# A windowed attention and two feed-forward layers on one core: where a softmax constant is added, which bank a product goes to, who issues two stores

## The chip, the cores and the metric

The kernel runs on one core of a Trainium2 chip. A core has a matrix engine (TensorE, PE in the profile, with its weight loads listed apart as PEld), three elementwise engines (VectorE or DVE, ScalarE or ACT, GpSimd or POOL) and SyncE (SP), which here only issues DMAs. Each engine works through its own queue of instructions in order. The metric is the device time of one execution in microseconds (us); the time before is the median of three runs.

## The reference: what is computed

All data is fp32. Attention over 4 batches, 8 heads, 576 positions, 64 values a head; each query sees the 128 keys up to its own, with a bias that falls with distance. The result, as 2304 rows of 512, goes through two layers.

```python
scores = scale * np.matmul(q, k.transpose(0, 1, 3, 2))
mask = (rel >= 0) & (rel < window)            # window = 128
scores = np.where(mask, scores + bias[None], -1000000000.0)
scores = scores - np.max(scores, axis=-1, keepdims=True)
attn = np.exp(scores)
attn = attn / (np.sum(attn, axis=-1, keepdims=True) + 1e-09)
x = np.matmul(attn, v)                        # rows (b, s), columns (h, d)
h = x @ w_in                                  # 512 x 2048
g = np.where(h > 0.0, h, np.exp(np.minimum(h, 0.0)) - 1.0)
x = g @ w_out                                 # 2048 x 512
h = x @ w_in_2
out = np.maximum(0.01 * h, h) @ w_out_2
```

The `1e-09` added to the sums is what the change's title calls the constant.

## The kernel before

**Products.** TensorE has to keep fp32 accuracy, so every product of a layer is three matmuls: both operands are split into a high and a low part (`fp32r`), and high x high, high x low and low x high are added in one accumulator (`split_mm`, whose matmul is line 120). The low part is what VectorE gets by subtracting the high part from the fp32 value: where av, the attention's result, lies in PSUM, ScalarE casts it to the high part (`values_cast`) and VectorE subtracts (`values_rest`). Both write `x`, the left operand of layer 1, and both read the bank that av lies in. The weights come as 64-bit words in pieces of 512 KB (`w_in`, `w_out`) and are converted to fp32 and split by ScalarE and VectorE (`wraw` is what was loaded, `wf` the first step of ScalarE, line 170, and `w` the result).

**Stages.** The attention is cut into steps: a step `s` is a pair of heads with up to two groups of queries (its `subs`, one or two) of a block of 256 rows. A step goes through `score_mm` (s_ps on TensorE), `score_min` (VectorE: bias, mask and maximum, the `stat` of the rows), `score_exp` (ScalarE: exp, with the row sums into `stat`), the constant, `score_rec` (VectorE: reciprocal), `score_norm` (GpSimd: the multiply `t<-t,stat`), `transposes` (TensorE into `pt_ps`, then ScalarE's copy to `pt`), `selects` (GpSimd: sets to zero what is outside the window) and `values` (TensorE: av_ps from `pt` and V).

In the opening, 16 steps (`FIRST`) run in an order written out by hand: while `Ordered.on` is set, every instruction of `act`, `dve` and `pool` keeps the order of the program on its engine. Round `n` has the transposes of step n, the products of step n - 1, the reductions, exp and constant of step n + 2, the selects of step n, and the multiply of step n + 1. Conversions of early weight pieces are mixed in on ScalarE and VectorE (`EARLY`).

After it, layer 1 runs over five blocks J of rows (512, 256, 512, 512, 512), each over 16 chunks c of 128 of the 2048 hidden values: `mlp1_h` (h_ps, 12 matmuls, then exp on ScalarE, and on VectorE a minimum, the maximum of line 522 that reads the bank last, and the subtract for the low part) and `mlp1_y` (the second product, two chunks later). At some chunks, the starts (at J = 0 chunks 3, 7, 11 and 15, then every other chunk from 0), two attention steps of a later block stand ahead of h_ps: their transposes, the values of the pair before, their selects and the scores of the next pair. After the last chunk of a block, `ys` copies (even pieces by ScalarE, odd ones by VectorE, in buffers `eg` that the chunks also use, three of them) go to DRAM as `x2T`, four stores of 256 KB. Layer 2 loads them again (`xr`), and its `mlp2_h` and `mlp2_y` run to the end; the `g` of its chunks (line 681) is made by ScalarE from h_ps, in the same `eg` buffers. The first chunks of layer 2 are mixed into the last block of layer 1, and the last two blocks' stores are issued by ScalarE, all others by SyncE.

**Order.** TensorE and the conversions of the weights keep the program's order. Outside the opening a scheduler puts the other instructions in order, and buffers of a pool are given out in turn: who asks for a buffer waits for the last reader of what lay in it.

**Banks.** PSUM has eight banks: s0 and s1 (scores; s1 also the first transposes of a start), h and c, y0 to y3. The second transposes of a start go into h, av of the late blocks into c (line 458), and h_ps alternates between h and c:

```python
        tag = "s0" if last and cs[0] < LAG2 and (LAG2 - cs[0]) % 2 else "h"
        if not last and cs[0] % 2 == (J == 0):
            tag = "c"
```

So before, the h_ps of a chunk with a start goes to c (even chunks from J = 1 on, odd ones at J = 0), and that of a chunk without one to h.

Of the kernel before, what the change touches and what calls it, by code (L numbers as in the profile page):

```python
# [84 lines left out]
def attention_elu_leaky_kernel(  # L85
# [262 lines left out]
    def score_exp(s):  # L348
        st = steps[s]
        t, stat = st["t"], st["stat"]  # L350
        for i, (t0, n, before, hh, c) in enumerate(st["reg"]):
            act.activation(t[:n, c], t[:n, c], AF.Exp, scale=-1.0,
                           bias=stat[:n, 0, i:i + 1], accum_out=stat[:n, 1, i:i + 1])
        nq, m = st["subs"][0][1], len(st["reg"])
        if Ordered.on:
            act.activation(stat[:nq, 1, :m], stat[:nq, 1, :m], AF.Copy, bias=1e-9)
        else:
            dve.tensor_scalar(stat[:nq, 1, :m], stat[:nq, 1, :m], 1e-9, None, op0=ALU.add)
# [12 lines left out]
    def scores(k):  # L371
# [5 lines left out]
        for s in (2 * k, 2 * k + 1):  # L377
            score_min(s)
            score_exp(s)
            score_rec(s)  # L380
            score_norm(s)
# [61 lines left out]
    def values(s):  # L443
# [17 lines left out]
        for t0, n, hh, k0, nk, c in st["parts"]:  # L461
            ch = [x[0] for x in chunks].index(k0)
            nth = sum(x[0] == -nk and x[2] == hh for x in mms)
            mms.append((-nk, nth, hh, ch, slice(t0 + off, t0 + off + n), c))


        mms.sort(key=lambda x: x[:3])
        for i, (nk, _, hh, ch, q, c) in enumerate(mms):
            matmul(av[hh * D:hh * D + D, q], v[:-nk, ch, hh * D:hh * D + D], pt[:-nk, c],
                   start=st["first"] and all(x[2] != hh for x in mms[:i]),  # L470
# [17 lines left out]
    def mlp1_h(J, cs, late_work=lambda: None):  # L488
# [8 lines left out]
        tag = "s0" if last and cs[0] < LAG2 and (LAG2 - cs[0]) % 2 else "h"  # L497
        if not last and cs[0] % 2 == (J == 0):

# [29 lines left out]
    def mlp1_y(J, cs, gg):  # L529
# [12 lines left out]
        if cs[-1] == NC - 1:  # L542
            for i, y in enumerate(Y.pop(J)):
# [5 lines left out]

                q = nc.sync if J < len(BLK1) - 2 else nc.scalar  # L550
                q.dma_start(out=x2T[:, i * per:i * per + per, t0:t0 + n], in_=ys)
# [36 lines left out]
    score_min(0)  # L588
    score_exp(0)
    score_min(1)  # L590
    score_rec(0)
    score_norm(0)
    score_exp(1)
    for n in range(FIRST):
        m = n + 2
# [7 lines left out]
        score_min(m)  # L603
        if n < FIRST - 2:
            score_norm(m - 1)
        score_exp(m)
        selects(n)
        if n >= FIRST - 2:
            score_norm(m - 1)
# [18 lines left out]
    for J in range(len(BLK1) - 1):  # L628
# [3 lines left out]
        for c in range(NC):  # L632
            if c in starts:
                transposes(2 * done + 1, "s1")
                transposes(2 * done, "h")
                values_to(2 * done - 1)
# [167 lines left out]
```

## Time and profile before

| | |
|---|---|
| median of three runs | 944.99 us (943.14 to 945.45) |
| profiled execution, its own time | 949.66 us |
| its span | 948.0 us |
| mean granted clock of TensorE | 0.988 |
| PE busy | 97% of the span |
| VectorE, ScalarE, GpSimd busy | 43%, 43%, 12% |

The profiled execution is one of the program with the hardware profiler on, and all rows below are of it. Its span runs from the first to the last instruction; the time includes what lies around that. An instruction's row has the start and the duration in microseconds, the engine, the line in the code, what it writes and reads, shapes, and how many of its kind in a row; in square brackets stands how long the engine was idle before it and which instruction ended that. L111 is the line of the wrapper `Ordered` and L120 that of `matmul`, so rows of these lines are told apart by the names of the tiles.

### The profile page before, as it was taken

Reading aid. Unit: us, or ns where it says so; the run is one execution under the profiler, and the core shown is the slowest. Engines: PE = TensorE matmul, PEld = TensorE weight load, DVE = VectorE, ACT = ScalarE, POOL = GpSimd, SP = SyncE. Lnnn points to the kernel's source line nnn. Section 1 sums busy time; section 2 is a strip of 40 time slices with the busy share of each in tenths; the row PEclk is TensorE's granted clock in tenths of the full one; section 3 lists DMA queues with packets and bytes.
Section 4 is the critical chain, followed back from the end, with each engine's and each line's share of the span. In section 5 each row is a group of like instructions: output and inputs, shape, how many; then the busy total and the mean of one; then the engine's idle time right before and its main releaser. Section 6 shows DMA issues by size and latency. Waiting matters only on the chain.

```text
span 948.0 us, 12963 instructions
## 1 busy us (share of the span) xinstructions
PE 923.8 (97%) x4885; PEld 752.4 (79%) x4885; DVE 408.8 (43%) x1035; ACT 405.0 (43%) x918; POOL 115.6 (12%) x281
## 2 busy tenths in 40 slices
PE   8799999999999999999999998999999999999998
PEld 5468887998877777787888887888888888888886
DVE  5878965656544444443476665211211121111111
ACT  6877864444343443332376665322322232222222
POOL 4611122322222211221000000000000000000000
PEclk9979999999999999999999998999999999999999
DMA  9940422321210120100444334010110010001001
GB/s 287 353 174 16 141 67 69 89 67 49 65 45 23 43 82 27 46 9 1 156 157 146 124 128 157 1 67 1 45 44 1 1 45 1 0 1 45 1 1 45
DMA packets 41759, 66.77 MB, mean 70 GB/s; under 512 B 3680, under 2 KB 27232, under 8 KB 41696
## 3 DMA queue, kind: packets, MB, share of 16 engines
q1 hardware_dynamic: 40400, 63.72, 20.2%
q10 hardware_dynamic: 1296, 2.23, 0.6%
q8 instruction: 38, 0.62, 0.3%
q14 instruction: 25, 0.20, 0.1%
HBM read 56.49 MB, written 9.44 MB: 70 GB/s over the span
## 4 chain that ended last, share of the span: by engine, by line
PE 90%; ACT 3%; DMA 3%; DVE 2%; issue 1%; SPq 1%; POOL 0%; ACTq 0%; DVEq 0%
PE h_ps L120 42%; PE y L120 20%; PE o_y L120 18%; PE av_ps L120 3%; PE s_ps L120 2%; DMA wraw<-in_w_in 2%; PE pt_ps L411 2%; PE o_s L120 1%; PE o_c L120 1%; ACT pt L417 1%; DVE x L111 1%; DMA x2T<-ys 1%; ACT wraw L175 0%; ACT x L111 0%; ACT t L111 0%
## 5 line engine op out<-in xcount | busy, mean ns | idle before, releaser
L120 PE MATMUL h_ps<-x,w 128*128 128x512 f32 (+1 forms) x1920 | 431.4, 374 | 8.8 <-DVE x L111 3.7
L120 PEld LDWEIGHTS h_ps<-x,w 128*128 128x128 f32 x1920 | 340.0, 191 | 80.7 <-DVE x L111 12.2
L686 DVE TENSOR_TENSOR g2l<-g,g2h 128x512 fp32r<-128x512 f32 (+1 forms) x80 | 51.0, 637 | 270.1 <-ACT g2h L685 270.1
L120 PE MATMUL o_y<-w,g2h 128*128 128x512 f32 x512 | 157.9, 389 | 0.0
L120 PE MATMUL y<-gh,w 128*128 128x512 f32 (+1 forms) x640 | 157.5, 368 | 0.0
L681 ACT ACTIVATE g<-h_ps 128x512 f32<-128x512 f32 (+1 forms) x80 | 44.2, 554 | 255.9 <-PE h_ps L120 255.9
L120 PEld LDWEIGHTS y<-gh,w 128*128 128x128 f32 x640 | 113.9, 189 | 20.4 <-DVE ys L546 0.3
L120 PEld LDWEIGHTS o_y<-w,g2h 128*128 128x128 f32 x512 | 96.4, 188 | 20.1
L120 PE MATMUL o_y<-w,g2l 128*128 128x512 f32 x256 | 99.6, 389 | 0.0
L520 ACT ACTIVATE eg<-h_ps 128x512 f32<-128x512 f32 (+1 forms) x80 | 44.0, 551 | 88.8 <-PE h_ps L120 86.2
L111 ACT ACTIVATE t<-t,stat 128x128 f32<-128x128 f32 (+2 forms) x160 | 62.6, 394 | 45.3 <-DVE t L111 30.3
L111 POOL TENSOR_SCALAR t<-t,stat 128x128 f32<-128x128 f32 (+3 forms) x160 | 66.9, 431 | 101.1 <-DVE stat L111 91.3
L120 PE MATMUL y<-gl,w 128*128 128x512 f32 (+1 forms) x320 | 78.7, 368 | 0.0
L523 ACT CAST gh<-eg 128x512 fp32r<-128x512 f32 (+1 forms) x80 | 46.2, 578 | 74.2 <-DVE eg L522 67.5
L111 POOL TENSOR_SCALAR_AFFINE_SELECT pt<-pt 128x256 f32<-128x256 f32 (+1 forms) x112 | 47.2, 429 | 221.0 <-ACT pt L417 217.2
L524 DVE TENSOR_TENSOR gl<-eg,gh 128x512 fp32r<-128x512 f32 (+1 forms) x80 | 51.3, 641 | 38.8 <-ACT gh L523 38.6
L120 PEld LDWEIGHTS y<-gl,w 128*128 128x128 f32 x320 | 56.9, 189 | 10.0
L521 DVE TENSOR_SCALAR eg<-eg 128x512 f32<-128x512 f32 (+1 forms) x80 | 32.6, 408 | 72.1 <-ACT eg L520 70.1
L120 PEld LDWEIGHTS o_y<-w,g2l 128*128 128x128 f32 x256 | 48.0, 188 | 10.0
L111 DVE CUSTOM_DVE_ANT_0 t<-s_ps,bias 128x256 f32<-128x256 f32 (+4 forms) x160 | 51.8, 370 | 2.9 <-PE s_ps L120 2.8
L522 DVE TENSOR_TENSOR eg<-h_ps,eg 128x512 f32<-128x512 f32 (+1 forms) x80 | 50.9, 638 | 2.5
L685 ACT CAST g2h<-g 128x512 fp32r<-128x512 f32 (+1 forms) x80 | 46.3, 578 | 2.3
(58 smaller groups left out, 678.7 us busy)
## 6 DMA issues: line engine op xcount, KB each, us to landing
wraw<-in_w_in SPq DMA_DIRECT2D x32, 512.0 KB, 3.8
wraw<-in_w_out SPq DMA_DIRECT2D x32, 512.0 KB, 4.8
qkr<-in_kT SPq DMA_DIRECT2D x28, 192.0 KB, 2.9
xr<-x2T SPq DMA_DIRECT2D x4, 1024.0 KB, 5.4
qkr<-in_qT SPq DMA_DIRECT2D x28, 128.0 KB, 2.6
out<-os SPq DMA_DIRECT2D x14, 256.0 KB, 2.2
vr<-in_vp SPq DMA_DIRECT2D x16, 192.0 KB, 2.5
x2T<-ys SPq DMA_DIRECT2D x10, 256.0 KB, 2.3
```

The lines of the kernel that those rows point to most:

```text
L111: ins = f(*args, **kw)
L120: tc.keep_in_program_order(nc.tensor.matmul(*args, **kw))
L411: tc.keep_in_program_order(nc.tensor.transpose(ps[:nk, col:col + n], t[:n, c:c + nk], ident[:n, :n]))
L417: tc.keep_in_program_order(nc.scalar.copy(pt[:nk, c], ps[:nk, c]))
L520: nc.scalar.activation(g[:, :m], ps, AF.Exp)
L521: nc.vector.tensor_scalar(g[:, :m], g[:, :m], 1.0, -1.0, op0=ALU.min, op1=ALU.add)
L522: nc.vector.tensor_tensor(g[:, :m], ps, g[:, :m], op=ALU.max)
L523: nc.scalar.copy(hi[:, :m], g[:, :m])
L524: nc.vector.tensor_tensor(lo[:, :m], g[:, :m], hi[:, :m].bitcast(F32), op=ALU.subtract)
L681: nc.scalar.activation(g, ps, AF.Prelu, alpha=0.01)
L685: nc.scalar.copy(hi, g)
L686: nc.vector.tensor_tensor(lo, g, hi.bitcast(F32), op=ALU.subtract)
```

## The change

Six small edits, which the title of the change counts as four and one.

1. The constant gets a function of its own, `score_eps`. In the opening it is an instruction of GpSimd (`tensor_scalar`, add and a multiply by one) where it was one of ScalarE (`activation` with Copy and a bias), and in round n it is issued behind `selects(n)`. Outside the opening it stays on VectorE.
2. `values` puts the products with 64 keys ahead of those with 128 (`nk` ascending).
3. The test of parity of the h bank is turned round: a chunk with a start now uses h, one without uses c.
4. Of the last two blocks' x2T stores the odd pieces go to SyncE, the even ones stay on ScalarE.
5. In round 14 the multiply (`score_norm`) comes ahead of the selects, as in the rounds before it; only round 15 keeps it behind.
6. At a start the two transposes are sorted by their number of `subs`: the step with fewer goes first and into s1; where they are equal, the even step goes first.

```diff
+    def score_eps(s):
+        st = steps[s]
+        stat = st["stat"]
         nq, m = st["subs"][0][1], len(st["reg"])
         if Ordered.on:
-            act.activation(stat[:nq, 1, :m], stat[:nq, 1, :m], AF.Copy, bias=1e-9)
+            pool.tensor_scalar(stat[:nq, 1, :m], stat[:nq, 1, :m], 1e-9, 1.0, op0=ALU.add, op1=ALU.mult)
         else:
             dve.tensor_scalar(stat[:nq, 1, :m], stat[:nq, 1, :m], 1e-9, None, op0=ALU.add)
...
-            nth = sum(x[0] == -nk and x[2] == hh for x in mms)
-            mms.append((-nk, nth, hh, ch, slice(t0 + off, t0 + off + n), c))
+            nth = sum(x[0] == nk and x[2] == hh for x in mms)
+            mms.append((nk, nth, hh, ch, slice(t0 + off, t0 + off + n), c))
...
-        if not last and cs[0] % 2 == (J == 0):
+        if not last and cs[0] % 2 != (J == 0):
...
-                q = nc.sync if J < len(BLK1) - 2 else nc.scalar
+                q = nc.sync if J < len(BLK1) - 2 or i % 2 else nc.scalar
...
         score_min(m)
-        if n < FIRST - 2:
+        if n < FIRST - 1:
             score_norm(m - 1)
         score_exp(m)
         selects(n)
-        if n >= FIRST - 2:
+        score_eps(m)
+        if n == FIRST - 1:
             score_norm(m - 1)
...
-                transposes(2 * done + 1, "s1")
-                transposes(2 * done, "h")
+                for s, tag in zip(sorted((2 * done, 2 * done + 1), key=lambda s: len(steps[s]["subs"])), ("s1", "h")):
+                    transposes(s, tag)
```

In the rows of the orders below, a row is the line, the operation, what it writes and reads, and its shape.

GpSimd at the end of the opening, before (rounds 12 to 15; `t<-t,stat` is the multiply, `pt<-pt` the selects):

```order
L111 AFFINE_SELECT pt<-pt 128x256 x2
L111 TENSOR_SCALAR t<-t,stat 128x128 x2
L111 AFFINE_SELECT pt<-pt 128x256 x4
L111 TENSOR_SCALAR t<-t,stat 128x128 x2
L111 AFFINE_SELECT pt<-pt 128x256 x2
L111 TENSOR_SCALAR t<-t,stat 64x128 x2
```

The same place after (`stat<-stat` is the constant):

```order
L111 TENSOR_SCALAR stat<-stat 128x2
L111 TENSOR_SCALAR t<-t,stat 128x128 x2
L111 AFFINE_SELECT pt<-pt 128x256 x2
L111 TENSOR_SCALAR stat<-stat 128x2
L111 TENSOR_SCALAR t<-t,stat 128x128 x2
L111 AFFINE_SELECT pt<-pt 128x256 x2
L111 TENSOR_SCALAR stat<-stat 64x4
L111 AFFINE_SELECT pt<-pt 128x256 x2
L111 TENSOR_SCALAR stat<-stat 128x2
L111 TENSOR_SCALAR t<-t,stat 64x128 x2
```

The constant stands behind each round's selects, and the multiply that stood behind four selects in a row, those of rounds 13 and 14, now stands between them.

ScalarE where layer 1's last block but one ends and its last begins, before (`ys` copies, the x2T stores, then `wf` and `wraw` of a weight piece and the first `g` of layer 2):

```order
L548 COPY ys<-y_4815 128x512
L548 COPY ys<-y_4817 128x512
L551 DMA x2T<-ys 128x512 x4
L170 ACTIVATE wf<-wraw 128x1024
L175 ACTIVATE wraw<-wraw 128x1024
L681 ACTIVATE g_5790<-h_ps 128x512
```

ScalarE there after:

```order
L553 COPY ys<-y_4815 128x512
L553 COPY ys<-y_4817 128x512
L556 DMA x2T<-ys 128x512 x2
L170 ACTIVATE wf<-wraw 128x1024
L175 ACTIVATE wraw<-wraw 128x1024
L690 ACTIVATE g_5790<-h_ps 128x512
```

And SyncE there after:

```order
L673 DMA xr<-x2T 128x4x512
L159 DMA wraw<-in_w_in 128x1024
L159 DMA wraw<-in_w_out 128x1024
L556 DMA x2T<-ys 128x512 x2
L673 DMA xr<-x2T 128x4x512
```

ScalarE has two stores instead of four; the other two stand on SyncE behind the loads of a weight piece and ahead of an `xr` load.

TensorE at a start of layer 1 with a step of one group, before, with what each waits for:

```order
L411 MATMUL pt_ps<-ident,t 128x128 [waits Pool_49] x2
L411 MATMUL pt_ps<-ident,t 128x128 [waits DVE_49]
L411 MATMUL pt_ps<-ident,t 128x128
L411 MATMUL pt_ps<-ident,t 64x128 x2
L120 MATMUL av_ps<-pt,vr 64x128 [waits DMAHW7_49]
L120 MATMUL av_ps<-pt,vr 64x128
L120 MATMUL av_ps<-pt,vr 64x128 [waits DMAHW6_49]
L120 MATMUL av_ps<-pt,vr 64x128 x5
L120 MATMUL s_ps<-qkr 128x192 [waits DMAHW5_49,DMAHW4_49]
L120 MATMUL s_ps<-qkr 128x192 [waits Activation_49]
L120 MATMUL s_ps<-qkr 128x256 x2
L120 MATMUL h_ps<-x_2788,w_4_877 128x512 [waits DVE_49]
```

The same start after:

```order
L416 MATMUL pt_ps<-ident,t 128x128 [waits Pool_49] x2
L416 MATMUL pt_ps<-ident,t 64x128 x2
L416 MATMUL pt_ps<-ident,t 128x128 [waits DVE_49,Pool_49]
L416 MATMUL pt_ps<-ident,t 128x128 [waits Pool_49]
L120 MATMUL av_ps<-pt,vr 64x128 [waits DMAHW6_49,DVE_49]
L120 MATMUL av_ps<-pt,vr 64x128
L120 MATMUL av_ps<-pt,vr 64x128 [waits DMAHW7_49]
L120 MATMUL av_ps<-pt,vr 64x128 x5
L120 MATMUL s_ps<-qkr 128x192 [waits DMAHW5_49,DMAHW4_49]
L120 MATMUL s_ps<-qkr 128x192 [waits PE_49,Activation_49]
L120 MATMUL s_ps<-qkr 128x256 x2
L120 MATMUL h_ps<-x_2788,w_4_877 128x512 [waits Activation_49]
```

The first h_ps of the start waited for VectorE and now waits for ScalarE; av waits for VectorE, which it did not; and the transposes of the step with 64 rows have moved up.

## Rows read from the trace of the kernel before

**Rows 1.** The page: busy time of each engine, share of the span, instructions.
```profile
PE 923.8 (97%) x4885; PEld 752.4 (79%) x4885; DVE 408.8 (43%) x1035; ACT 405.0 (43%) x918; POOL 115.6 (12%) x281
```
**Rows 2.** Windows: stretch, length, each engine's busy time (instructions), clock, DMA share, GB/s.
```profile
0.00:47.53 47.53, 38.45 (x281) 22.43 (x281) 33.81 (x136) 36.03 (x124) 26.42 (x65) 0.97 0.92 320
...
600.00:943.50 343.50, 343.50 (x1528) 284.76 (x1526) 56.15 (x84) 87.27 (x149) 0.00 (x0) 1.00 0.05 18
```
**Rows 3.** Windows of the three stretches with the low clock.
```profile
45.25:51.50 6.25, 5.77 (x19) 3.91 (x19) 2.03 (x8) 2.77 (x8) 4.08 (x11) 0.50 0.82 325
65.75:72.25 6.50, 6.50 (x19) 4.81 (x18) 4.45 (x19) 4.35 (x14) 1.50 (x5) 0.50 0.18 52
584.50:591.00 6.50, 5.45 (x13) 4.29 (x14) 5.39 (x8) 5.24 (x8) 0.00 (x0) 0.50 0.00 0
```
**Rows 4.** Timeline, PE: the four longest waits, in order of time.
```profile
45.73 0.82 PE L411 MATMUL pt_ps<-ident,t 128*128 128x128 f32 x2 [2.25 <-POOL t L111]
...
65.33 0.91 PE L120 MATMUL s_ps<-qkr 64*64 64x192 f32 x6 [1.77 <-ACT pt L417]
...
437.78 3.02 PE L120 MATMUL h_ps<-x,w 128*128 128x512 f32 x12 [1.21 <-DVE x L111]
...
585.55 5.49 PE L120 MATMUL h_ps<-x,w 128*128 128x512 f32 x12 [3.28 <-ACT g L681]
```
**Rows 5.** Waits of weight loads, 60 to 460 us: total us, times, longest us.
```profile
PEld h_ps L120 <- DVE x L111: 11.9, 23, 1.4
```
**Rows 6.** Timeline of one start of layer 1, 365 to 369 us.
```profile
365.77 0.63 PEld L120 LDWEIGHTS s_ps<-qkr 64*128 64x128 f32 x8 [0.17 <-issue]
...
365.94 0.63 ACT L417 COPY pt<-pt_ps 128x256 f32<-128x256 f32 x2 [0.21 <-PE av_ps L120]
...
366.88 0.42 DVE L111 TENSOR_TENSOR x<-av_ps,x 128x256 fp32r<-128x256 f32 x1 [2.49 <-ACT x L111]
...
367.36 0.76 PEld L120 LDWEIGHTS h_ps<-x,w 128*128 128x128 f32 x4 [0.96 <-DVE x L111]
```
**Rows 7.** Timeline, weight loads of another start.
```profile
265.81 0.52 PEld L120 LDWEIGHTS s_ps<-qkr 64*64 64x64 f32 x8 [0.33 <-issue]
```
**Rows 8.** Timeline, VectorE's maximum ahead of a start in the 256-row block.
```profile
223.54 0.42 DVE L522 TENSOR_TENSOR eg<-h_ps,eg 128x256 f32<-128x256 f32 x1
```
**Rows 9.** Timeline of the step from layer 1 to layer 2.
```profile
575.46 0.43 SPq L159 DMA_DIRECT2D wraw<-in_w_out  x1
...
576.71 6.12 ACTq L551 DMA_DIRECT2D x2T<-ys  x4
...
581.77 0.69 DVE L546 COPY ys<-y 128x512 f32<-128x512 f32 x1 [4.77 <-DMA x2T<-ys]
...
582.87 1.12 ACT L170 ACTIVATE wf<-wraw 128x1024 f32<-128x1024 f32 x1 [5.71 <-DVE ys L546]
...
584.91 0.86 ACT L681 ACTIVATE g<-h_ps 128x512 f32<-128x512 f32 x2
```
**Rows 10.** DMA issues, 574 to 579 us: KB each, median us to landing.
```profile
wraw<-in_w_out SPq DMA_DIRECT2D x1, 512.0 KB, 5.5
```
**Rows 11.** Timeline, end of the opening: constant, copy of transposes 15, first h_ps.
```profile
44.98 0.21 ACT L111 ACTIVATE stat<-stat 64x4 f32<-64x4 f32 x1
...
46.59 0.37 ACT L417 COPY pt<-pt_ps 128x256 f32<-128x256 f32 x1 [1.40 <-PE pt_ps L411]
...
47.53 4.21 PE L120 MATMUL h_ps<-x,w 128*128 128x512 f32 x9
```
**Rows 12.** Timeline, GpSimd: selects of 256 and of 128 columns.
```profile
25.30 0.88 POOL L111 TENSOR_SCALAR_AFFINE_SELECT pt<-pt 128x256 f32<-128x256 f32 x2 [0.27 <-ACT pt L417]
...
94.22 0.66 POOL L111 TENSOR_SCALAR_AFFINE_SELECT pt<-pt 128x128 f32<-128x128 f32 x2 [18.37 <-ACT pt L417]
```
**Rows 13.** Timeline of round 10 of the opening: selects, and VectorE's reciprocal.
```profile
33.11 1.68 POOL L111 TENSOR_SCALAR_AFFINE_SELECT pt<-pt 128x256 f32<-128x256 f32 x2 [0.36 <-ACT pt L417]
...
34.45 0.15 DVE L111 RECIPROCAL stat<-stat 128x2 f32<-128x2 f32 x1
```

More of the change, by code (lines that the diff above doesn't have):

```diff
@@ L379, in scores @@
             score_exp(s)
+            score_eps(s)
             score_rec(s)
@@ L462, in values @@
             ch = [x[0] for x in chunks].index(k0)
-            nth = sum(x[0] == -nk and x[2] == hh for x in mms)
-            mms.append((-nk, nth, hh, ch, slice(t0 + off, t0 + off + n), c))
+            nth = sum(x[0] == nk and x[2] == hh for x in mms)
+            mms.append((nk, nth, hh, ch, slice(t0 + off, t0 + off + n), c))
         mms.sort(key=lambda x: x[:3])
         for i, (nk, _, hh, ch, q, c) in enumerate(mms):
-            matmul(av[hh * D:hh * D + D, q], v[:-nk, ch, hh * D:hh * D + D], pt[:-nk, c],
+            matmul(av[hh * D:hh * D + D, q], v[:nk, ch, hh * D:hh * D + D], pt[:nk, c],
                    start=st["first"] and all(x[2] != hh for x in mms[:i]),
@@ L589, in attention_elu_leaky_kernel @@
     score_exp(0)
+    score_eps(0)
     score_min(1)
@@ L593, in attention_elu_leaky_kernel @@
     score_exp(1)
+    score_eps(1)
     for n in range(FIRST):
```

## The prediction

> **What bounds the kernel now.** I read the page's busy times first, then the busy time by stage, then the granted clock, then what the weight loads wait for, and only then single stretches. PE is busy 923.8 of 948.0 us [rows 1], and from 600 to 943.5 us it has no idle time at all [rows 2], so nothing outside PE's own work can be saved there. What is left lies in three places: the opening up to 47.53 us, where PE is idle 9.1 us [rows 2]; the starts of layer 1 between there and 460 us; and the step from layer 1 to layer 2 around 585 us. [...] The list of waits says for whom the weight loads, which go ahead of their matmuls, stood between 60 and 460 us: 11.9 us in 23 waits for `x` from VectorE [rows 5]. So the edits that can pay are those at these 23 h chunks and at the layer step.
>
> **The change part by part.** All of it is counted against the profiled execution (949.66 us, span 948.0). That one is 4.7 us above the median of 944.99; I carry the differences over to the median unchanged.
>
> *The parity of the h bank.* Where a chunk opens with transposes, values and scores, PE runs transposes, av, s_ps, h_ps. Before, this h_ps went into bank c, which the av of the same start had just filled, so it waited for ScalarE's cast of av and VectorE's subtract. One start shows it: the weight loads of s_ps end at 366.40, the subtract runs from 366.88 to 367.30, the h weights load at 367.36, 0.96 us late [rows 6]. There are 23 such waits, 11.9 us in all, 1.4 us the longest [rows 5]. After it the h_ps of a start goes into bank h and waits for the copy of the second transposes, which in that start ends at 366.57 [rows 6]. What stays is the change of shape on PE, 0.17 us before the loads of s_ps there [rows 6], 0.33 in another start [rows 7]. Bounds: 11.9 - 23 x 0.33 = 4.3, and 11.9 if h_ps has no such gap. I take 0.20 (the row's 0.17, and the copy can be a little late): 11.9 - 4.6 = **-7.3 us**. PE is otherwise full there, so it goes through to the end. What the new placement asks: av now goes into c, which held the chunk before, whose last reader is VectorE's max. It is tightest in the 256-row block: there the max ends at 223.96 [rows 8] and the transposes, which waited for the same max already, go ahead of av and cover it. Cost nothing; if the cover is gone, some tenths at each of eight starts.
>
> *The order of transposes and of av.* Same instructions. The first copy then waits for the av that read its buffer first, not last, so it comes earlier; it is behind no wait that I have not counted. Putting the 64-key products first takes away one change of shape at four starts (0.17 each) and adds one at as many others: 0, bounds ±0.7.
>
> *The x2T stores.* At the layer step ScalarE copies ys 0 and 2, and its queue is then held from 576.71 for 6.12 us by its four stores: store 3 waits for VectorE's copy of ys 3, which waits at 581.77 for a free eg buffer, that is for store 0 to land. ScalarE is free at 582.83, does wf and wraw, and g at 584.91 frees the bank [rows 9]: h_ps at 585.55 [rows 4]. After, it issues stores 0 and 2 alone and is free at about 577.6. Then wf waits for its piece: w_out was issued at 575.46 [rows 9] and took 5.5 us [rows 10], so 580.96. From wf to g it is 2.04 us and from g to h_ps 0.64, so h_ps at 583.64 instead of 585.55: 1.9 us. The g buffer is free when store 1 lands: issued by SyncE at about 577.1, some 5.1 us as store 0, 582.2, sooner than g. Store 3 queues on SyncE and holds only a later xr load. The idle time left is 1.37 us, nearer to the 1.21 that left the clock alone than to the 1.77 that did not. So I also count the slow h_ps back, 5.49 us for twelve [rows 4] that take half of it at the full clock: 2.7. **-4.6 us**; bounds -6.0 (no wait at all) and 0 (g held by store 1). Layer 1's next to last block has the same stores, but no h_ps behind them waits for g: 0.
>
> [...]
>
> *The constant on GpSimd.* Eighteen small instructions leave ScalarE; one takes 0.21 us there [rows 11]. On GpSimd no row has this operation. Its size follows from selects: 0.44 us at 256 columns, 0.33 at 128 [rows 12], so 0.22 for next to none; upper bound 0.33. With 0.06 for each handing over, as from the subtract to the h weights [rows 6], it is 0.34 on the chain from exp to reciprocal against 0.21 and 0.03: +0.10 a round, of which ScalarE's shorter queue gives some back. Then it stands behind the selects, and two of those take 1.68 us instead of 0.88 [rows 12, 13] beside VectorE's long two-input subtract: in the row they end at 34.79, so the reciprocal comes at 35.07, not at 34.45 [rows 13], with the next reduction queued behind it. Three rounds do so (8, 10, 12), some 0.5 each net. **+1.6 us** at reciprocal 15; bounds -0.5 and +4.
>
> [...]
>
> *The multiply in round 14 ahead of the selects.* Before, transposes 15 waited for GpSimd's multiply, which stood behind selects 14: transposes at 45.73 [rows 4], their copy at 46.59, h_ps at 47.53 [rows 11]. After, the transposes come early and ScalarE sets the time: it is through with exp 16 at 44.98, where the constant stood, and from the copy to h_ps it is 0.94 [rows 11]: 45.92, **-1.6 us**. The two edits cancel: h_ps at about 47.5. PE's wait is split, before av 14 (which waits for the selects now) and before h_ps; I leave the clock falling as before: **0** for the opening, bounds -3 (full clock, by half of the slow stretch's matmuls) and +3. The wait that ends at 65.33 hangs on ScalarE's copy, which none of the edits brings sooner; it stays.
>
> **Sum:** -7.3 - 4.6 + 0 = -11.9 us; 944.99 - 11.9 = **933 us**.
>
> **The rivals.**
> 1. *The layer step gives only part.* A store that lands late or a clock that falls all the same: -0.8 to -1.9 there; -7.3 - 0.8 = -8.1, 937 us. For it: the clock fell behind 1.77 us.
> 2. *The opening keeps its clock.* -3 more: 930 us. For it: the single wait of 2.25 us is split; against: PE does little between the two.
> 3. *The h chunks only change what they wait for*, the copy on ScalarE at each start, 0.33 to 0.4 left: -3 there, 938 us. For it: that copy ends only 0.17 us behind the weight loads of s_ps [rows 6].
> 4. *Slower: the chain through GpSimd.* The constant is on the chain of each of 16 rounds. If one costs d, the opening grows by 16 x (d - 0.22); it eats the 11.9 us from d = 0.96 us. Beside VectorE's subtract a select has taken 0.84 us [rows 13], so it is not out of reach, but two columns are: 947 us at d = 1.1.
> 5. *The change does not act* (waits merely renamed, stores as late): 945 us.
>
> **How the numbers follow.** Chances: forecast 0.48, rival 1 0.20, rival 2 0.15, rival 3 0.10, rival 4 0.03, rival 5 0.04. The range runs from rival 2 less 1 us to rivals 1 and 3 together (-5): 929 to 940 us. About 0.3% (2.8 us) is what a measurement of this kernel can tell from no change. The forecast and rivals 1 to 3 all lie beyond it, so faster 0.92; a little of each may not, so same 0.05, slower 0.03.
>
> **What the changed profile would show.** Weight loads of h_ps waiting for `x` gone from the list, with issue gaps of 0.17 in their place; right above 6 us saved between 59 and 460, wrong below 4. At the layer step g near 583.0 less what was saved before, and twelve h_ps in 2.7 us. In the opening stat on GpSimd at 0.2 us, reciprocals drifting from round 10 on, transposes 15 about 1 us sooner, the first h_ps at 47 to 48. A stat of 0.5 us or more, or a new wait of av for VectorE, would make the prediction wrong.

## The result, and the profile after

The changed kernel takes 936.38 us (median of four runs, 936.15 to 937.65) where the kernel before took 944.97 (943.14 to 945.45): 8.6 us less, a ratio of 0.9914 with a 95% interval of 0.9898 to 0.9930. Forecast were 933 us, 11.9 us less, in a range of 929 to 940. The direction and the range hold; the size was 3.3 us too large.

The profiled execution has its own time of 936.15 us and a span of 934.4, 13.6 us less than the 948.0 of before. So 5 of these 13.6 us are not in the medians. The runs made later say why: 29 executions of the kernel before had granted clocks from 0.986 to 0.997, 0.995 in the middle, and times from 942.55 to 950.37 us. The profiled one of before, with 0.988 and the three stretches of [rows 3], was among the slowest; the four of the changed kernel had 0.996 to 0.998. Below, a low clock is a reading of 0.50 in the clock column and the full clock one of 1.00; windows that lie across both read in between.

Busy times of the page, answering [rows 1]:

```profile
PE 915.1 (98%) x4885; PEld 747.9 (80%) x4885; DVE 409.0 (44%) x1035; ACT 400.8 (43%) x900; POOL 124.8 (13%) x299
```

Windows of the changed kernel: the opening and the last 343.5 us, answering [rows 2], and the one stretch with a low clock, answering [rows 3] (columns as there):

```profile
0.00:47.53 47.53, 37.59 (x277) 21.74 (x277) 33.06 (x130) 32.02 (x105) 31.88 (x79) 0.96 0.92 319
...
586.50:930.00 343.50, 343.50 (x1529) 285.06 (x1528) 56.17 (x84) 87.27 (x149) 0.00 (x0) 1.00 0.05 17
...
8.00:12.00 4.00, 4.00 (x24) 2.39 (x20) 1.64 (x11) 2.21 (x10) 2.81 (x8) 0.57 0.98 344
```

The last stretch is as full as it was. GpSimd has 18 instructions more and ScalarE 18 less. The three stretches of [rows 3] are gone, and the column reads 0.50 once, from 8.3 to 11.7 us. TensorE is busy all through that window, yet nothing is lost by it that can be seen: the opening's reciprocal 4 (counted from 0, as the steps) comes at 13.73 us here and at 14.04 in the last run below, which has no such stretch. At the very start the clock column says less than it seems to. It shows 1.00 there in both kernels, but the same four s_ps matmuls take 0.80 us before and 0.49 after:

```profile
5.72 0.80 PE L120 MATMUL s_ps<-qkvr 64*128 64x128 f32 x4 [0.34 <-DMA qkvr<-in_kT]
```

```profile
5.53 0.49 PE L120 MATMUL s_ps<-qkvr 64*128 64x128 f32 x4 [0.34 <-DMA qkvr<-in_kT]
```

In the trace of before the longer durations go on to about 11 us: four pt_ps of 256 columns take 1.03 us at 9.15 and 0.61 at 11.52, four s_ps 0.49 at 11.09. In the changed kernel the eight s_ps at 3.72 take 1.47 us, 1.66 before, and those at 5.53 are already at 0.49.

Timeline of TensorE, answering [rows 4]: the waits ahead of the first h_ps, of s_ps at the first start, of an h_ps at 428 and at the layer step.

```profile
47.31 0.91 PE L120 MATMUL av_ps<-pt,qkvr 128*64 128x128 f32 x8 [1.36 <-POOL pt L111]
48.15 2.34 PE L120 MATMUL h_ps<-x,w 128*128 128x512 f32 x9
...
63.78 1.18 PE L120 MATMUL s_ps<-qkr 64*64 64x192 f32 x10 [1.58 <-ACT pt L422]
...
428.39 1.89 PE L120 MATMUL h_ps<-x,w 128*128 128x512 f32 x7 [0.55 <-ACT pt L422]
...
575.01 3.04 PE L120 MATMUL h_ps<-x,w 128*128 128x512 f32 x12 [1.36 <-ACT g L690]
```

The multiply no longer holds the transposes; av waits for the selects instead, 1.36 us in place of 2.25. The first h_ps starts 0.6 us later than before, but its nine matmuls take 2.34 us instead of 4.21 [rows 11].

What the weight loads of h_ps wait for between 60 and 460 us, answering [rows 5]:

```profile
PEld h_ps L120 <- ACT x L111: 3.3, 10, 0.3
PEld h_ps L120 <- issue: 2.8, 10, 0.3
...
PEld h_ps L120 <- ACT pt L422: 0.8, 1, 0.8
```

No wait for VectorE is left. 6.9 us in 21 waits stay: sixteen are 0.33 us each, four 0.17 to 0.22 and one 0.79. The start that answers [rows 6], timeline of the weight loads:

```profile
357.85 1.04 PEld L120 LDWEIGHTS s_ps<-qkr 64*128 64x128 f32 x8 [0.17 <-issue]
...
359.22 1.91 PEld L120 LDWEIGHTS h_ps<-x,w 128*128 128x128 f32 x9 [0.33 <-issue]
```

Before, the wait at that place was 0.96 us. The layer step, answering [rows 9]:

```profile
567.47 1.08 ACT L553 COPY ys<-y 128x512 f32<-128x512 f32 x2 [2.40 <-PE y L120]
...
568.08 0.81 ACTq L556 DMA_DIRECT2D x2T<-ys  x2
568.41 5.76 SPq L556 DMA_DIRECT2D x2T<-ys  x2
569.00 1.12 ACT L170 ACTIVATE wf<-wraw 128x1024 f32<-128x1024 f32 x1 [0.46 <-ACT ys L553]
...
573.12 0.69 DVE L551 COPY ys<-y 128x512 f32<-128x512 f32 x1 [4.74 <-DMA x2T<-ys]
...
574.36 0.87 ACT L690 ACTIVATE g<-h_ps 128x512 f32<-128x512 f32 x2 [3.22 <-DMA x2T<-ys]
```

From ScalarE's first ys copy to h_ps it is 7.54 us (567.47 to 575.01) where it was 9.46: 1.92 us less, to the tenth what was forecast. But g waits for something else than forecast: `wf` had its piece at once, and g then waited 3.22 us for a store to land, since its buffer is one that `ys` had. The store is the second that ScalarE itself issued, piece 2, which lands at 574.28; SyncE's store of piece 1 had landed at 574.05. The issues of the two, 568.42 to 568.90 us (KB each, us to landing):

```profile
x2T<-ys SPq DMA_DIRECT2D x1, 256.0 KB, 5.6
x2T<-ys ACTq DMA_DIRECT2D x1, 256.0 KB, 5.7
```

ScalarE's queue is no longer held; SyncE's is, for 5.76 us, by the same wait for VectorE's copy of ys 3.

### The profile page after: what moved, and what is told of

Its sections match the earlier page's. It is cut to its first block, busy times and chain, and to the rows that moved or that the text cites. A ratio compares the mean times of both kernels' runs of the same rounds, so it can differ in the third digit from the quotient of the medians.

```text
span 934.4 us, 13060 instructions
## 1 busy us (share of the span) xinstructions
PE 915.1 (98%) x4885; PEld 747.9 (80%) x4885; DVE 409.0 (44%) x1035; ACT 400.8 (43%) x900; POOL 124.8 (13%) x299
## 4 chain that ended last, share of the span: by engine, by line
PE 90%; ACT 2%; DVE 2%; DMA 2%; POOL 1%; issue 1%; SPq 1%; ACTq 0%; DVEq 0%; POOLq 0%
PE h_ps L120 41%; PE y L120 20%; PE o_y L120 19%; PE s_ps L120 4%; PE av_ps L120 3%; PE pt_ps L416 1%; PE o_s L120 1%; PE o_c L120 1%; DMA x2T<-ys 1%; DMA wraw<-in_w_out 1%; POOL pt L111 1%; DVE t L111 1%; ACT t L111 0%; ACT w L111 0%; POOL t L111 0%
## 5 line engine op out<-in xcount | busy, mean ns | idle before, releaser
L120 PE MATMUL h_ps<-x,w 128*128 128x512 f32 (+1 forms) x1920 | 424.7, 371 | 3.3 <-ACT g L690 1.4
L120 PEld LDWEIGHTS h_ps<-x,w 128*128 128x128 f32 x1920 | 335.8, 188 | 71.9 <-ACT x L111 4.0
L111 POOL TENSOR_SCALAR t<-t,stat 128x128 f32<-128x128 f32 (+3 forms) x160 | 70.1, 452 | 89.3 <-DVE stat L111 81.0
```

Of the source, the lines that this page charges most:

```text
L111: ins = f(*args, **kw)
L120: tc.keep_in_program_order(nc.tensor.matmul(*args, **kw))
```

## The experiments

Each part was made alone on the kernel before, then single parts were undone or added on the changed one. Two measures are used: the median, which holds the clock's falls as they come, and the length of stretches between two marks in the trace, which at the full clock repeats to 0.3 us (297.84 to 298.09 from the first to the fourth block in four of the kernels below). The marks are reciprocal 6 of the opening, the first h_ps, ScalarE's first ys copy of the first, fourth and fifth block, the h_ps that waits at the layer step, and the end of the span. A star stands where TensorE's granted clock read below 1.00 in part of the stretch (the end of the span behind the last matmul is left out).

| kernel | reciprocal 6 to first h_ps | to first block | first to fourth block | fourth to fifth | to the layer step's h_ps | to the end |
|---|---|---|---|---|---|---|
| before | 28.67* | 115.44* | 297.84 (162.97 to 460.81) | 115.28 | 9.46* | 362.40* |
| parity alone | 28.38* | 110.73* | 293.10 | 115.26 | 9.42* | 361.30* |
| stores alone | 28.54* | 111.40* | 297.94 | 115.94 | 7.50 | 359.41 |
| constant alone | 30.66* | 114.91* | 298.09 | 115.31 | 9.45 | 359.84 |
| round 14 alone | 26.88 | 110.31 | 297.91 | 115.31 | 9.37 | 361.39* |
| orders alone | 28.66* | 113.88* | 297.48 | 115.29 | 9.28 | 361.35* |
| the change | 28.44 | 109.53 | 293.74 | 116.05 | 7.54 | 359.43 |

Ahead of reciprocal 6 the opening does not repeat: it comes at 18.73 to 19.72 us in the profiles of kernels with the constant on ScalarE, at 19.23 to 20.04 in those with it on GpSimd. So absolute times in the opening are compared with care below.

**The parity alone.**

```diff
-        if not last and cs[0] % 2 == (J == 0):
+        if not last and cs[0] % 2 != (J == 0):
```

> The kernel before with the parity of the h bank alone turned round. Theory A (the prediction's): the 11.9 us for which the h weight loads waited all lie on the path, so 7.3 us less, about 937.5 us. Theory B: only TensorE's own idle time counts, 3.7 us in 8 waits for x from VectorE in the list of before, since the other waits of the weight loads lie beside matmuls that still run; with the change of shape that stays, 3 to 4 us less, about 941.5 us. Both expect no h weight load that waits for VectorE's subtract.

Measured: 939.49 us against 945.49, ratio 0.9942 (0.9918 to 0.9966), 6.0 us less; 4.74 us of it between the first and the fourth block. The waits that stay, in the list of weight loads:

```profile
PEld h_ps L120 <- issue: 3.5, 12, 0.3
PEld h_ps L120 <- ACT x L111: 2.0, 6, 0.3
...
PEld h_ps L120 <- ACT pt L417: 1.4, 3, 0.7
```

They add up to 6.9 us in 21, so 11.9 - 6.9 = 5.0 us went from the weight loads between 60 and 460. The median lies between the two theories, and its interval of 2.3 us either way holds both; the stretches decide. TensorE's own idle time before was 3.7 us, and more than that was won: 4.74 us from the first to the fourth block, and 0.8 more at the starts ahead of them (110.31 us for round 14 alone, 109.53 for the change, both at the full clock). So theory A's way of counting holds, with 0.33 us left at most starts where 0.20 was taken. That these 0.33 us are the change of shape is argued from their constant size, also at the ten places where nothing was waited for, and from where such pauses stand: between 60 and 460 us of the changed profile 88 of the 91 pauses of 0.15 us or more between two weight loads are at a change of shape. No run varies the shape, and not every change has such a pause: from the 64 x 64 loads of s_ps to the 128 x 128 of h_ps it is 0.07 us at four starts.

**The stores alone.**

```diff
-                q = nc.sync if J < len(BLK1) - 2 else nc.scalar
+                q = nc.sync if J < len(BLK1) - 2 or i % 2 else nc.scalar
```

> The kernel before with the stores' queue alone changed. Theory A (the prediction's): g about 1.9 us sooner, PE's wait 1.3 to 1.4 us instead of 3.28, no low clock behind it, so the next twelve h_ps in about 3 instead of 5.5 us: 4.6 us less, about 940.4 us. Rival: the clock falls all the same, 1.9 us less, about 943 us; by the issue time alone 0.8 us less.

Measured: 941.49 us, ratio 0.9955 (0.9938 to 0.9972), 4.0 us less. Timeline: after the fourth block, and at the layer step.

```profile
460.79 0.50 PE L120 MATMUL y<-gh,w 128*128 128x512 f32 x1 [0.50 <-DVE ys L546]
...
579.41 0.87 ACT L681 ACTIVATE g<-h_ps 128x512 f32<-128x512 f32 x2 [3.17 <-DMA x2T<-ys]
...
580.07 2.11 PE L120 MATMUL h_ps<-x,w 128*128 128x512 f32 x8 [1.32 <-ACT g L681]
```

The interval of the median holds theory A and the rival both; the trace decides. The wait is 1.32 us and the clock column stays at 1.00 behind it, from 550 to 600 us, as theory A has it. A new wait stands after the fourth block: VectorE's copy of ys 3 comes later, and `y` waits 0.50 us for its bank; the stretch is 0.66 us longer.

**The constant alone.** It moves to GpSimd behind the selects, as in the first two pieces of the change's diff.

> The kernel before with the constant of the opening on GpSimd behind the selects, alone. Theory A (the prediction's): reciprocal 15 some 1.6 us later, and with the multiply of round 15 still behind two pairs of selects the whole of it goes to the first h_ps: 1.6 us more, about 946.6 us. The trace of after has reciprocal 15 2.5 us later than before, so theory B: 2.5 us more, 947.5 us. Both expect the low clock ahead of the first h_ps as before. A third: ScalarE's shorter queue gives it back, 0.

Measured: 948.55 us, ratio 1.0029 (1.0013 to 1.0045), 3.1 us more. Timeline of the end of the opening and of the layer step:

```profile
45.98 2.11 POOL L111 TENSOR_SCALAR_AFFINE_SELECT pt<-pt 128x256 f32<-128x256 f32 x2 [1.07 <-ACT pt L422]
48.18 0.19 POOL L111 TENSOR_SCALAR stat<-stat 64x4 f32<-64x4 f32 x1
...
48.89 0.83 PE L416 MATMUL pt_ps<-ident,t 128*128 128x128 f32 x2 [2.87 <-POOL t L111]
...
588.46 3.04 PE L120 MATMUL h_ps<-x,w 128*128 128x512 f32 x12 [3.27 <-ACT g L689]
```

The single wait ahead of the first h_ps grows from 2.25 to 2.87 us. From reciprocal 6 to the first h_ps it is 2.0 us more than before (30.66 against 28.67); the rest of the 3.1 lies ahead of reciprocal 6 and in falls of the clock, and what of it is the edit's stays open. In this execution the clock did not fall at the layer step behind 3.27 us of waiting (1.00 from 560 to 595 us), and the twelve h_ps took 3.04 us: the price of the fall in other executions is the difference to this number, 2.45 us for the 5.49 of [rows 4].

**Round 14 alone.**

```diff
-        if n < FIRST - 2:
+        if n < FIRST - 1:
             score_norm(m - 1)
...
-        if n >= FIRST - 2:
+        if n == FIRST - 1:
             score_norm(m - 1)
```

> The kernel before with the multiply of round 14 ahead of the selects, alone. Theory A (the prediction's): the first h_ps 1.6 us sooner with the clock as before, 943.4 us. Theory B: the single wait of 2.25 us is split, the clock stays at its full level and nine h_ps take 2.3 instead of 4.2 us: 3.5 us or more less, 941.5 us or below. A third: the wait moves to av, which stands behind the selects, and nothing is won.

Measured: 942.77 us, ratio 0.9968 (0.9953 to 0.9982), 2.7 us less. Timeline:

```profile
45.75 0.92 PE L120 MATMUL av_ps<-pt,qkvr 128*64 128x128 f32 x8 [1.21 <-POOL pt L111]
...
46.59 2.34 PE L120 MATMUL h_ps<-x,w 128*128 128x512 f32 x9
```

Both theories have part of it. The first h_ps comes 0.9 us sooner, though this execution was already 0.9 us late at reciprocal 6 (19.72 against 18.86); from there it is 1.8 us sooner (26.88 against 28.67). And the nine matmuls run at the full clock, 1.00 up to 59.4 us, in 2.34 us where [rows 11] have 4.21. Over all profiles the clock fell to 0.50 between 45 and 47.5 us, ahead of the first h_ps, in the five kernels without this edit, and read 1.00 there in all nine with it.

**The orders alone.** Transposes of a start and products of `values`, as in the change's diff.

> The kernel before with the two orders alone: transposes of a start by the number of groups, products of values with 64 keys first. The prediction's theory: changes of shape saved and added cancel, 0, bounds 0.7 us either way. Rival, from the stretches between the ends of layer 1's blocks, where the changed kernel needs 0.6 us more over three blocks than the kernel with the parity alone: about 0.6 us slower.

Measured: 944.07 us against 945.27, ratio 0.9985 (0.9964 to 1.0007): no difference that can be told, and from the first to the fourth block 0.36 us less, not 0.6 more.

**The constant back on ScalarE, all else changed.**

```diff
-            pool.tensor_scalar(stat[:nq, 1, :m], stat[:nq, 1, :m], 1e-9, 1.0, op0=ALU.add, op1=ALU.mult)
+            act.activation(stat[:nq, 1, :m], stat[:nq, 1, :m], AF.Copy, bias=1e-9)
...
+        score_eps(m)
         selects(n)
-        score_eps(m)
```

> The changed kernel with the constant of the opening on ScalarE again, right behind exp; all other edits stay. If the constant on GpSimd costs what it costs alone (3.06 us in the run of that edit by itself), this one is 3 us faster than the changed kernel, about 933.4 us. If the two edits of the opening hide each other's price (the prediction had them cancel, 1.6 us each), 1.6 us faster, 934.8 us. If the queue of ScalarE is what counts, no gain.

Measured: 935.15 us, ratio to before 0.9886 (0.9866 to 0.9906), 1.2 us less than the changed kernel. The median alone is nearest to the second theory. Timeline:

```profile
45.90 2.33 PE L120 MATMUL h_ps<-x,w 128*128 128x512 f32 x9
...
61.53 1.71 PE L120 MATMUL s_ps<-qkr 64*64 64x192 f32 x10 [1.58 <-ACT pt L422]
...
63.17 4.01 PE L120 MATMUL h_ps<-x,w 128*128 128x512 f32 x12
```

The first h_ps comes 2.25 us sooner than in the changed kernel, and so does s_ps; 0.68 of that is there at reciprocal 6 already (19.03 against 19.71), and 1.57 come behind it (26.87 against 28.44). So the second theory's 1.6 us is what the rounds show. But behind the same wait of 1.58 us the clock falls here, to 0.50 from 62.0 to 65.0 us, and did not there (1.00 from 60 to 70): twelve h_ps take 4.01 us, 3.04 there, and the stretch to the first block 1.5 us more (111.04 against 109.53). Of 2.25 us the end keeps 1.0 in the two profiles. That became the next question.

**The constant on GpSimd, ahead of the selects.**

```diff
+        score_eps(m)
         selects(n)
-        score_eps(m)
```

> The changed kernel with the constant of the opening on GpSimd, but ahead of the selects of the round instead of behind them. If the price is the place in GpSimd's queue (behind the selects), most of the 3 us comes back: 933.5 to 934.5 us. If the price is the way to GpSimd and back, nothing comes back; and if the selects now wait for exp, av comes later and it is slower than the changed kernel, 937 us or more.

Measured: 940.48 us, ratio to before 0.9945 (0.9924 to 0.9965), 4.1 us slower than the changed kernel. Timeline:

```profile
27.86 0.19 POOL L111 TENSOR_SCALAR stat<-stat 128x2 f32<-128x2 f32 x1 [1.27 <-ACT t L111]
...
28.12 0.88 POOL L111 TENSOR_SCALAR_AFFINE_SELECT pt<-pt 128x256 f32<-128x256 f32 x2
...
28.58 0.91 PE L120 MATMUL av_ps<-pt,qkvr 128*64 128x128 f32 x8 [1.21 <-POOL pt L111]
```

The second branch of the expectation: GpSimd stands 1.27 us for exp with the selects behind it, and av waits 1.21 us for those. From reciprocal 6 to the first h_ps it is 30.03 us, 1.6 more than in the change. Not all of the 4.1 us is this: the clock also fell behind the wait at the first start here (0.50 from 68 to 70 us, twelve h_ps in 4.60 us), as it did not in the profile of the change. Of the two places in GpSimd's queue the change has the better one.

**No constant in the opening.**

```diff
-            pool.tensor_scalar(stat[:nq, 1, :m], stat[:nq, 1, :m], 1e-9, 1.0, op0=ALU.add, op1=ALU.mult)
+            pass
```

> The changed kernel without the constant in the opening's 18 steps: the reciprocal reads the sums as exp left them. This shows all that the constant can cost wherever it stands. Theory: 16 rounds with no handing over, so at least the 3 us of the edit alone and up to 16 times 0.2 us more: 930.5 to 933.4 us. If something else (GpSimd's selects ahead of av, VectorE) sets the rounds, it stays at 935 to 936 us.

Measured: 933.78 us, ratio to before 0.9868 (0.9845 to 0.9891), 2.6 us less than the changed kernel, 0.4 above the upper end of the first theory. Here too the clock falls behind the wait at the first start, 1.56 us: 0.50 from 62 to 64 us, twelve h_ps in 4.61. From reciprocal 6 to the first h_ps it is 25.85 us without the constant, 26.87 with it on ScalarE, 28.44 with it on GpSimd: over these ten rounds it costs 1.0 us on ScalarE and 2.6 on GpSimd, 0.1 and 0.26 a round.

**Odd stores on SyncE in the last block alone**, with the constant on ScalarE.

```diff
-                q = nc.sync if J < len(BLK1) - 2 or i % 2 else nc.scalar
+                q = nc.sync if J < len(BLK1) - 2 or J == len(BLK1) - 1 and i % 2 else nc.scalar
```

> The changed kernel with the constant on ScalarE again and with the odd stores on SyncE in layer 1's last block alone. In the traces of the changed kernel and of the stores' edit alone, a second product of the block after next to last waits 0.5 us for VectorE's copy of ys 3, and the stretch between the two blocks' ends is 0.7 to 0.8 us longer than before. Theory: that wait goes and 0.7 us with it, 934.4 us where the kernel with both odd pairs on SyncE had 935.15. Rival: the wait is covered later, no difference.

Measured: 934.07 us, ratio to before 0.9880 (0.9856 to 0.9903). The stretch from the fourth to the fifth block is 115.25 us where the kernel with both odd pairs on SyncE had 115.99: 0.74 us, as expected. So it is the fourth block's odd stores on SyncE that bring the new wait for `ys`.

**Work in the wait at the first start**, on top of that kernel: 12 matmuls of the identity into a part of the scores' bank that is written again later; their results are not used.

```diff
+                if fill:
+                    warm(ps[0][:, BLK:], fill)
+                    fill = 0
...
-        ps = score_mm(2 * k)
+        ps = score_mm(2 * k, fill=12 if k == FIRST // 2 + 1 else 0)
```

> The kernel of the run f1_last_block, with 12 matmuls of the identity (results not used) in TensorE's wait of 1.58 us at the first start of layer 1. Theory: that wait is where the clock falls in this kernel, at a price of some 1.6 us; with work in it the clock stays up, 1 to 2 us faster than f1_last_block, about 933 us. Rival: the clock falls at another place or the matmuls delay the scores, no difference or up to 0.5 us slower.

Measured: 932.67 us (932.34 to 933.23), ratio to before 0.9867 (0.9845 to 0.9889), the fastest of all medians. Timeline of the same place without the fill, then with it:

```profile
61.95 1.66 PE L120 MATMUL s_ps<-qkr 64*64 64x192 f32 x10 [1.55 <-ACT pt L422]
63.54 4.06 PE L120 MATMUL h_ps<-x,w 128*128 128x512 f32 x12
```

```profile
60.07 1.48 PE L120 MATMUL s_ps<-ident 128*128 128x256 bf16 x12
61.72 1.18 PE L120 MATMUL s_ps<-qkr 64*64 64x192 f32 x10 [0.17 <-ACT pt L425]
62.82 3.01 PE L120 MATMUL h_ps<-x,w 128*128 128x512 f32 x12
```

The clock stays up, 1.00 from 60 to 70 us against 0.83 without the fill, and 1.4 us are won, as the theory has it.

**The orders as before**, otherwise as the run of the last block alone.

> The kernel of the run f1_last_block with the two orders (transposes of a start, products of values) as before the change. From the ends of layer 1's blocks: the parity alone took 293.1 us from the first to the fourth, the changed kernel 293.7, so the orders cost 0.6 us and this one is 0.6 us faster than f1_last_block. From the run of the orders alone (1.2 us faster than before, interval with 1 in it) the opposite, 1.2 us slower. The prediction's theory: no difference.

Measured: 933.49 us, ratio to before 0.9874 (0.9851 to 0.9897), 0.6 us less than 934.07 with ranges that overlap (932.68 to 934.54 and 932.30 to 934.86). First to fourth block 293.07 us against 293.50. By the medians this is no difference. By the stretches the orders cost 0.4 us with the new parity and saved 0.4 with the old one (297.48 against 297.84); why the sign turns was not looked into.

**The same fill in the changed kernel as it is.**

> The changed kernel as it is, with the same 12 matmuls of the identity in TensorE's wait at the first start of layer 1. Theory: in the changed kernel the clock did not fall behind that wait, so nothing is won (within 0.3 us of 936.4); the constant then costs some 2.3 us, and the kernel with it on ScalarE showed only 1.2 us of that because there the clock fell. Rival: the changed kernel loses its clock there in most executions too, 1.4 us faster, 935 us, and the constant costs 1.2 us in every case.

Measured: 936.03 us (935.25 to 936.47), 0.35 less than the changed kernel. Windows at that stretch:

```profile
60.00:70.00 10.00, 9.86 (x59) 7.45 (x58) 9.57 (x29) 10.00 (x25) 1.54 (x2) 1.00 0.12 36
```

Nothing is won to speak of, as the theory has it. With the fill in both, the medians put the constant on GpSimd at 936.03 - 932.67 - 0.74 (the stores of the fourth block) = 2.6 us, but they are not quite of one scale: the kernel before took 944.71 us beside the one and 946.72 beside the other. The profiles, both without a fall there, put it at 1.9: 1.58 us from reciprocal 6 to the first h_ps (28.46 against 26.88) and 0.32 from the first to the fourth block (293.77 against 293.45), the latter without a cause that was found. The 1.2 us of the kernel with the constant on ScalarE was short by a fall of the clock. Why the clock fell behind that wait of 1.58 us in one kernel and not in the other stays open.

## Why the prediction came out as it did

*The parity.* Right in mechanism, 5.5 us in the stretches (6.0 in the medians) instead of 7.3. The step that was mis-sized is what stays per start: "I take 0.20", while 0.33 us, its other bound [rows 7], stayed at sixteen of 21 places. Rival 3 (the copy on ScalarE) is not what was seen: one wait for that copy is in the list, of 0.8 us (three in the parity alone, 1.4 together), and the rest has the same 0.33 or less. That VectorE's maximum covers av held, apart from five waits of 0.2 to 0.3 us of av's weight loads for VectorE.

*The x2T stores.* Forecast 4.6, measured 4.0 us. The 1.9 us at the layer step came out as 1.92, but by luck in its reason: "Then wf waits for its piece" failed, and g was held by a store, as the bound of 0 had it, though by store 2 and not by store 1, which had landed 0.2 us before. That this store's landing lets g go 1.9 us sooner was in no step of the sum. The clock stayed up behind the shorter wait, 1.36 us, as chosen: 1.00 from 550 to 600 us (behind the 1.21 us that the choice leaned on it reads 1.00 too, from 437.78 to 445 us before). What that is worth was taken from the one profile with the most of it at 0.50: 5.49 us for twelve h_ps. In three others they took 4.54 to 4.61, in one 3.04 without a fall, so where 2.7 was taken the fall cost 2.45 us in this one, 1.5 in three, and in the fifth there was none. And "Layer 1's next to last block has the same stores ...: 0" failed: `y`, not h_ps, waits there, and it costs 0.7 us. No run shows the 0.8 us that the first rival counts and that the expectation of the stores' run has for the issue time alone: two stores take 0.81 us of ScalarE's queue after, but 1.9 us were won at the layer step, since that queue had stood most of its 6.12 us behind a wait and not behind issues.

*The constant.* Forecast 1.6 us at reciprocal 15, measured 2.46 there (44.59 against 42.13) and 3.1 us in the run of that edit alone. But 0.85 of the 2.46 is there at reciprocal 6, where the profiles scatter by a microsecond whatever the edit. From reciprocal 6 to 15 it is 24.88 us after and 23.27 before: 1.61 us, the forecast to the tenth, and the other profiles repeat both lengths to 0.03 us. First the rows of before, then GpSimd and VectorE after:

```profile
18.86 0.17 DVE L111 RECIPROCAL stat<-stat 128x2 f32<-128x2 f32 x1
...
42.13 0.17 DVE L111 RECIPROCAL stat<-stat 128x2 f32<-128x2 f32 x1 [0.85 <-ACT stat L111]
```

```profile
19.71 0.17 DVE L111 RECIPROCAL stat<-stat 128x2 f32<-128x2 f32 x1 [0.46 <-POOL stat L111]
...
28.94 1.70 DVE L111 CUSTOM_DVE_ANT_0 wraw<-wraw,wf 128x1024 uint16<-128x1024 uint16 x2
...
30.19 0.50 POOL L111 TENSOR_SCALAR stat<-stat 128x2 f32<-128x2 f32 x1
...
44.37 0.19 POOL L111 TENSOR_SCALAR stat<-stat 128x2 f32<-128x2 f32 x1 [0.27 <-ACT t L111]
44.59 0.17 DVE L111 RECIPROCAL stat<-stat 128x2 f32<-128x2 f32 x1 [0.89 <-POOL stat L111]
```

The way there is in part luck. The estimate of its size was good, 0.19 for 0.22. But in the three rounds where it runs beside one of VectorE's 0.89 us instructions (1.70 us for two in the row) it takes 0.50, which the sum left out, and in these the selects are late too. What the sum spread over three rounds of some 0.5 us came in five of 0.2 to 0.4, and the other four of the nine gave next to nothing. Rival 4's chain through GpSimd is what is seen, at 1.6 us instead of the 14 that its example had.

*Round 14.* "1.6 us sooner" came out as 1.8 (26.88 against 28.67 from reciprocal 6); that the forecast 45.92 is met by 45.90 in the kernel with the constant on ScalarE is luck, since that profile is 0.2 us late at reciprocal 6. "I leave the clock falling as before" failed, and rival 2 with it held: behind the split wait, 0.97 to 1.36 us ahead of av in seven profiles and 0.42 in the one of GpSimd ahead of the selects, the clock read 1.00 up to the first h_ps. "The two edits cancel" is right in the rounds: 28.44 us after, 28.67 before. In the medians of the edits alone (+3.1 and -2.7) both look larger, since these hold the clock and the start of the opening too.

*The sum.* By the medians of the parts alone it is -6.0 - 4.0 + 3.1 - 2.7 - 1.2 = -10.8, measured -8.6; each of these medians has an interval of 1.4 to 2.3 us either way. The stretches say more. Where both kernels can be read at the full clock, the change saves 0.8 us from the first h_ps to the first block, 4.1 to the fourth, 1.9 at the layer step and 0.4 behind it (359.84 for the constant alone, 359.43 after), and loses 0.8 between the fourth and the fifth block. With the 0.2 up to the first h_ps, which before has low clock in it, that is 6.7 us. The other 1.9 us of the measured 8.6 are left, by difference, for low clock that the changed kernel does not have, with the scatter ahead of reciprocal 6 and the result's own interval of 1.5 us in it. The forecast in the same terms was 9.2 and 2.7. So most of what it had too much is work at the full clock: 1.8 us at the starts, 0.8 at the fourth block's stores, and 0.6 from the first to the fourth block that the orders and the constant cost together (293.74 against 293.10 for the parity alone); 0.6 went the other way. The smaller part is "I carry the differences over to the median unchanged". The profile of before had three low stretches, the middle one of its executions had fewer or shorter ones (0.995 of clock against 0.988), so the median had less to win back.

*Its own signs.* "A stat of 0.5 us or more, or a new wait of av for VectorE, would make the prediction wrong": both are in the changed profile, three stats of 0.50 to 0.51 us and the five waits of av, and the prediction's range held all the same. Its mark "right above 6 us saved between 59 and 460, wrong below 4" leaves the 4.9 us of the stretches undecided. Transposes 15 came 0.2 us sooner (45.50 against 45.73) and not 1.

## What to carry to other kernels

In this kernel the waits of weight loads were the measure for a full TensorE, not its own idle time; what stays at a change of shape was best taken at its largest row. Before a fall of the clock goes into a sum, look at several executions: behind the wait at the first start it came in eight of twelve profiles, and one profile shows one draw. Stretches between marks that two traces share tell a change of a few microseconds better than absolute times or medians do. Here the small instruction moved to the freer engine took 0.19 us itself in most rounds and still cost 1.6 us from reciprocal 6 to 15: what stood ahead of it in that queue was late in some of the rounds.

## What the runs showed of the hardware that was not expected

The length of a wait did not decide here whether the clock fell. At the first start of layer 1 TensorE waits 1.55 to 1.78 us in twelve profiles; the column went to 0.50 in eight, from 0.3 us ahead of the wait's end to 2.0 us behind it, and stayed at 1.00 in four: the changed kernel after 1.58 us, the parity alone after 1.57, the stores alone after 1.78 and round 14 alone after 1.77. At the layer step it fell at 3.10 to 3.28 us in four profiles, and not at 3.27 in the fifth. With the shorter waits of the changed places it read 1.00 in every profile: at the layer step in the nine with the new stores (1.2 to 1.4 us of waiting in the four whose rows were read), and up to the first h_ps in the nine with the multiply of round 14 moved. The low stretches lasted 3.4 us (8.3 to 11.7 us of the changed profile) to 6.8 us (the first of [rows 3], with its edges); twelve h_ps at the layer step of the five kernels with the old stores took 3.04, 4.54, 4.61, 4.61 and 5.49 us.

In the opening the profiles fall into three groups, by what TensorE, busy for all of 8 to 10 us, starts there. In seven of fourteen, that of before among them, it is 9 or 10 instructions, with 1.00 in the clock column: four s_ps of 256 columns take 1.22 to 1.23 us at about 8 us, and in six whose rows go on four pt_ps take 1.03 to 1.04 us at 9.2 us or still at 11.9 (in two), where later ones take 0.61. In two, the parity alone and the changed kernel with the fill, it is 18 instructions, also at 1.00. In five, the changed kernel's among them, it is 12 to 15 at 0.57 to 0.74; in these the same four s_ps just ahead take 0.70 us, TensorE had waited 0.92 to 1.35 us at about 7 us, and the column reads 1.00 again by 14 us. A wait of 0.66 to 1.09 us at that place stands in the profiles of the first group and of the parity alone as well, with 1.00 behind it.

One instruction of two columns (once four) on GpSimd took 0.19 to 0.20 us fourteen times in the changed profile, twelve of them with no VectorE instruction beside it, and 0.41 to 0.51 us four times, beside VectorE instructions of 0.85 to 0.89 us: up to 2.6 times as long. A select of 256 columns took 0.40 us at the least and 1.62 at the most, the latter beside two VectorE subtracts of 0.68 us; with the constant alone two of them take 2.11 us at the end of the opening, against 0.88 in [rows 12].
